# The last stage of an attention and spectral-mix kernel, issued by a written list of steps

## The chip, the cores and the metric

The kernel runs on one core of a Trainium2 chip. The metric is the device time of one execution in microseconds (us). PE is the matrix engine, PEld its loading of stationary operands, DVE the vector engine, ACT the scalar engine, POOL the GpSimd engine, and SP the engine whose queue issues transfers here. PSUM is the memory that PE writes; a bank of it holds 512 f32 numbers in each of 128 partitions, and there are eight.

## The reference, cut to what matters

Causal attention over 8 batches, 8 heads, 576 positions and 64 columns gives x of 8 x 576 x 512. Then a spectral mix and a channel mix follow:

```python
X = np.fft.rfft(x, axis=1)
Y = np.zeros_like(X)
Xr, Xi = (np.real(X[:, :n_modes]), np.imag(X[:, :n_modes]))      # n_modes = 64
Yr = np.einsum('bmd,mde->bme', Xr, w_r) - np.einsum('bmd,mde->bme', Xi, w_i)
Yi = np.einsum('bmd,mde->bme', Xr, w_i) + np.einsum('bmd,mde->bme', Xi, w_r)
Y[:, :n_modes] = Yr + 1j * Yi
y = np.fft.irfft(Y, n=S, axis=1)
u = x + y
return (u + np.maximum(u @ w_ch, 0.0)).astype(np.float32)
```

The weights w_r and w_i are 64 x 512 x 512 each, 134 MB of f32 together, and are read once.

## The kernel before, in words

The order of all instructions is written out by hand (manual_schedule, line 91): each engine runs its own in the order in which the program issues them, and semaphores hold an instruction until what it reads is written and what it overwrites has been read.

The kernel has three stages. The first, up to line 464, is the attention for 32 pairs of heads, with the Fourier transform of each finished part and the first three quarters of the mode products (`modes`) in between. The weights come in through GpSimd's DMA queue (line 204), converted to bf16.

The second stage (lines 644 to 660) works on the last quarter of the modes in eight chunks. Each chunk gives a row block of the spectrum Y, `yb`, and through `y_transposed` and `y_times_wch` its product with w_ch, `vb`; both are put into the tile `yv` by a transfer on SP's queue. Between the chunks, `work()` prepares the last stage. The output is cut into 36 tiles of 128 rows, taken two at a time: 18 pairs, numbered 0 to 17. Pairs 4 and 10 hold the last 64 rows of four batches. For each of the pairs 2 to 17 ("kept"), `x_transposed` transposes x through PSUM, `x_times_wch` multiplies it by w_ch into two PSUM banks z, and `keep` copies this product to SBUF (`z1s`). Pairs 0 and 1 (NPRE = 2) keep theirs in PSUM.

The third stage uses u @ w_ch = x @ w_ch + y @ w_ch. For each pair it needs z, the kept product plus the inverse transform of Y w_ch (`add_y` with which = 1: two matmuls of 512 columns), and u, which is x (`start_u`: an identity matmul on x_all) plus the inverse transform of Y (`add_y` with which = 0). ACT takes the relu of z into a result tile (`relu`), DVE adds u from PSUM to it, one bank at a time (`finish`, line 635), and SP issues the output transfers (line 637). How the kept product enters z is set per pair by `ways` (line 486):

```python
ways = dict(zip(kept, "esesessesesseses"))
```

"e": the product is kept as a sum of two f16 tiles (one more DVE subtraction in `keep`, line 535), and PE adds both by four identity matmuls (line 687). "s": it is kept in f32, and ACT copies it into PSUM (line 683), on which PE accumulates. There are seven "e" and nine "s". The PSUM pools of this stage are `upool` and `auxpool` with two tiles of one bank, one per half of u for even and odd pairs, and `zpool` with two tiles of two banks. `seed(i + 1)` of an "s" pair is issued ahead of `relu(i)`; otherwise the loop at line 705 goes pair by pair.

Of the kernel before, what the change touches and what calls it, by code (L numbers as in the profile page):

```python
# [18 lines left out]
def kernel(  # L19
# [85 lines left out]
    auxpool = ctx.enter_context(tc.tile_pool(name="aux_psum", bufs=2, space=PSUM))  # L105
# [332 lines left out]
    with tc.tile_pool(name="sc_psum", bufs=2, space=PSUM) as scpool, \  # L438
# [25 lines left out]
        fft(N - 1)  # L464
    load(loads_w(len(wq)))
# [12 lines left out]
    ways = dict(zip(kept, "esesessesesseses"))  # L478
# [5 lines left out]
    upool = ctx.enter_context(tc.tile_pool(name="u_psum", bufs=2, space=PSUM))  # L484
    zpool = ctx.enter_context(tc.tile_pool(name="z_psum", bufs=2, space=PSUM))

# [17 lines left out]
    def x_transposed(i):  # L504
        xts[i] = xt_sb[len(xts) % 2]
        for x, (b, T) in enumerate(pairs[i]):
            ps = upool.tile([P, DT, P], FP32, name="xt_ps", tag="u")
            for rows, bb, ident in parts(b, T):
                for dt in range(DT):
                    nc.tensor.matmul(  # L510
                        ps[:, dt, rows], x_all[: rows.stop - rows.start, dt, bb, T, :],
                        ident, start=True, stop=True, skip_group_check=True,
                    )
            nc.vector.tensor_copy(out=xts[i][:, x], in_=ps)
# [83 lines left out]
    def start_u(i):  # L598
        pool, tag = ((upool, "u"), (auxpool, "aux"))[i % 2]
        us[i] = [pool.tile([P, DM], FP32, name="u_ps", tag=tag) for x in range(2)]  # L600
        for x, (b, T) in enumerate(pairs[i]):
            for r, bb, ident in parts(b, T):
                nc.tensor.matmul(  # L603
                    us[i][x][r, :].rearrange("p (g d) -> p g d", d=P), ident,
# [11 lines left out]
    def relu(i, parts_=1):  # L616
        rs[i] = result(i)
        for x in range(parts_):
            n = 2 // parts_
            nc.scalar.activation(  # L620
                out=rs[i][:, n * x : n * x + n], in_=zs[i][:, n * x : n * x + n], func=ACTF.Relu
            )

    def finish(i):
        if ways.get(i) == "v":
            rs[i] = result(i)
        for x, (b, T) in enumerate(pairs[i]):
            o = rs[i][:, x, :]
            if ways.get(i) == "v":
                nc.vector.tensor_tensor(out=o, in0=zs[i][:, x, :], in1=z1s[i][:, x, :], op=ALU.add)  # L630
                nc.vector.scalar_tensor_tensor(
                    out=o, in0=o, scalar=0.0, in1=us[i][x], op0=ALU.max, op1=ALU.add
                )
            else:
                nc.vector.tensor_tensor(out=o, in0=us[i][x], in1=o, op=ALU.add)
# [108 lines left out]
```

The softmax here doesn't subtract the row's maximum and nothing guards it: scores larger than these inputs give would overflow.

## Time and profile before

| What | us |
|---|---|
| median of 6 runs | 461.55 (461.26 to 461.84) |
| the profiled execution, its own time | 461.7 |
| span of its profile | 459.9 |
| first matmul of the products with the last block (line 594) | 424.60 |
| last matmul of the last stage starts | 454.51 |
| last DVE add ends | 456.36 |

All places in the profile are us from the span's start. In the stretches each engine has its busy time, the number of instructions in brackets, then PE's granted clock as a share of full speed, the DMA engines' busy share and the GB/s that they moved. A group's row gives line, engine and operation, output<-inputs, shapes, the count, the busy time, the mean ns of one, and the idle time of the engine just before it with what ended it. Two instructions of one engine overlap at their ends, so that a mean duration is a little longer than the distance from one to the next.

### The profile page before, as it was taken

The page shows a single profiled execution, that of the slowest core. Times are in us where ns is not written, and L with a number is a line of the kernel's source. Part 1 is how long each engine was busy: PE and PEld are TensorE (multiplying, and loading weights), DVE is VectorE, ACT ScalarE, POOL GpSimd, SP SyncE. Part 2 cuts the span into 40 slices and gives each one's busy share as a digit, 9 for nine tenths or more (in the row PEclk, how much of TensorE's full clock was granted, in tenths as well). Part 3 has the DMA queues.
Part 4 walks back from the last instruction along what each step waited for, and adds up shares of the span by engine and source line. Part 5 has one row for each costly group of instructions (what it writes and reads, how often), then busy time and mean ns, then how long its engine had stood idle before and what let it go on. Part 6 is the DMA issues. An engine that isn't in the chain of part 4 may idle for free.

```text
span 459.9 us, 10252 instructions
## 1 busy us (share of the span) xinstructions
PE 347.5 (76%) x4177; PEld 215.5 (47%) x4177; DVE 233.0 (51%) x519; ACT 218.2 (47%) x375; POOL 183.0 (40%) x269
## 2 busy tenths in 40 slices
PE   1879988974667779857666777567869858988995
PEld 1556656653445446644444544434544424444442
DVE  7775666662434346644333433334436625562675
ACT  1585875554444437744344434444422303340895
POOL 7755555544445455344544434434432223100000
PEclk9997999998777779998777977777798979999999
DMA  9999999999999999999999999999999999994697
GB/s 177 201 203 203 201 202 203 203 204 204 204 202 203 203 201 202 204 204 203 202 202 205 205 204 204 205 204 204 204 210 210 211 215 211 213 212 94 233 311 292
DMA packets 110063, 95.16 MB, mean 207 GB/s; under 512 B 28544, under 2 KB 105216, under 8 KB 110016
## 3 DMA queue, kind: packets, MB, share of 16 engines
q0 software_dynamic: 98960, 81.81, 112.4%
q1 hardware_dynamic: 11056, 12.70, 9.1%
q8 instruction: 33, 0.54, 0.4%
q14 instruction: 14, 0.11, 0.1%
HBM read 164.66 MB, written 9.44 MB: 379 GB/s over the span
## 4 chain that ended last, share of the span: by engine, by line
DMA 62%; PE 26%; DVE 6%; issue 3%; POOL 1%; ACT 0%; SPq 0%; DVEq 0%; POOLq 0%; ACTq 0%
DMA w_sb<-in_moe_w_i_dram 43%; DMA w_sb<-in_moe_w_r_dram 13%; DMA q<-in_q_dram 5%; PE z_ps L520 4%; PE sc_ps L342 3%; PE av_ps L371 3%; PE yp L416 2%; PE sc_ps L336 2%; PE z_ps L585 2%; PE u_ps L603 2%; PE u_ps L585 2%; PE tr_ps L301 2%; PE z_ps L687 1%; PE ft_ps L395 1%; DMA qtA<-ncum_sb 1%
## 5 line engine op out<-in xcount | busy, mean ns | idle before, releaser
L350 ACT ACTIVATE p_sb<-sc_ps,cumt_sb 128x576 f16<-128x576 f32 (+1 forms) x256 | 142.2, 634 | 59.6 <-PE sc_ps L342 59.4
L204 POOL DMA_DIRECT2D w_sb<-in_moe_w_i_dram x60 | 45.2, 753 | 76.3 <-DMA w_sb<-in_moe_w_i_dram 34.5
L204 POOL DMA_DIRECT2D w_sb<-in_moe_w_r_dram x60 | 45.1, 752 | 69.6 <-DMA w_sb<-in_moe_w_r_dram 26.3
L204 POOL DMA_DIRECT2D v<-in_v_dram x72 | 50.8, 707 | 35.8 <-DMA w_sb<-in_moe_w_i_dram 10.7
L301 PE MATMUL tr_ps<-ident,q 64*64 64x64 bf16 x576 | 18.7, 219 | 58.8 <-DMA q<-in_q_dram 58.1
L336 PE MATMUL sc_ps<-negm,ident 128*128 128x256 bf16 x256 | 58.1, 315 | 0.2
L416 PE MATMUL yp<-w_sb,xs 128*32 128x512 bf16 x480 | 39.8, 417 | 16.7 <-DMA w_sb<-in_moe_w_i_dram 12.2
L304 DVE COPY qtA<-tr_ps 64x576 bf16<-64x576 bf16 x32 | 23.8, 744 | 53.8 <-PE tr_ps L301 53.8
L321 ACT ACTIVATE p<-sc_ps,cumt 128x64 f16<-128x64 f32 x32 | 10.0, 313 | 84.5 <-PE sc_ps L317 84.5
L342 PE MATMUL sc_ps<-qtB,ktB 128*128 128x512 bf16 (+2 forms) x192 | 46.3, 360 | 0.0
L371 PE MATMUL av_ps<-v,p_sb 128*128 128x65 f16 x1024 | 45.7, 200 | 0.0
L304 DVE COPY ktA<-tr_ps 64x576 bf16<-64x576 bf16 x32 | 24.0, 749 | 42.4 <-PE tr_ps L301 42.4
L301 PEld LDWEIGHTS <-q 64*64 64x64 bf16 x576 | 14.8, 130 | 61.6 <-DMA q<-in_q_dram 60.6
L371 PEld LDWEIGHTS <-p_sb 128*128 128x128 f16 x1024 | 40.6, 102 | 5.1 <-issue 1.1
L342 PE MATMUL sc_ps<-qtA,ktA 65*128 65x512 bf16 (+2 forms) x192 | 38.1, 309 | 0.3 <-DMA qtA<-ncum_sb 0.3
L520 PE MATMUL z_ps<-wch_sb,xs 128*128 128x512 f16 x144 | 36.3, 399 | 0.7 <-ACT z L540 0.7
L376 DVE TENSOR_REDUCE den<-av_ps 128x5 f32<-128x10 f32 x64 | 10.8, 169 | 47.7 <-PE av_ps L371 47.7
L416 PEld LDWEIGHTS <-xs 128*32 128x32 bf16 x512 | 21.6, 172 | 27.4 <-issue 24.1
L381 DVE TENSOR_TENSOR x_all<-av_ps,rcp 128x320 f16<-128x320 f32 x64 | 31.5, 492 | 2.2
L342 PEld LDWEIGHTS <-ktB 128*128 128x128 bf16 x192 | 23.4, 122 | 16.4 <-issue 7.7
L304 ACT COPY ktB<-tr_ps 64x576 bf16<-64x576 bf16 x32 | 20.3, 634 | 20.3 <-DVE ktA L304 19.6
L301 PE MATMUL tr_ps<-ident,k 64*64 64x64 bf16 x576 | 17.6, 211 | 15.0 <-DVE qtB L304 9.1
(90 smaller groups left out, 497.4 us busy)
## 6 DMA issues: line engine op xcount, KB each, us to landing
w_sb<-in_moe_w_r_dram POOLq DMA_DIRECT2D x60, 512.0 KB, 11.9
w_sb<-in_moe_w_i_dram POOLq DMA_DIRECT2D x60, 512.0 KB, 11.9
q<-in_q_dram POOLq DMA_DIRECT2D x32, 144.0 KB, 9.7
k<-in_k_dram POOLq DMA_DIRECT2D x32, 144.0 KB, 10.0
v<-in_v_dram POOLq DMA_DIRECT2D x72, 64.0 KB, 10.0
out_dram<-r_sb SPq DMA_DIRECT2D x16, 256.0 KB, 2.7
out_dram<-r_w SPq DMA_DIRECT2D x16, 256.0 KB, 2.5
x_all<-in_moe_w_i_dram POOLq DMA_DIRECT2D x3, 512.0 KB, 9.8
```

The costliest lines, as they stand in the source:

```text
L204: nc.gpsimd.dma_start(out=dst, in_=src)
L301: nc.tensor.transpose(ps[rows, r, :], src[rows, r, :], ident16[rows, rows])
L304: copy(out=dst[n % NQ][rows, :].rearrange("d (p r) -> d p r", r=R), in_=ps[rows].rearrange("d r p -> d p r"),)
L336: nc.tensor.matmul(ps[:, bass.ds(w * S, W)], ident16, negm[:, bass.ts(r, W)], start=True, stop=False, skip_group_check=True,)
L342: nc.tensor.matmul(ps[:, c0 : c0 + i1 - i0], keys[:, w, r, :], qt[:, i0:i1], start=False, stop=True, skip_group_check=True,)
L350: nc.scalar.activation(out=pt[:, poff[x] : poff[x] + S - w * W], in_=ps[:, w * S : (w + 1) * S - w * W], func=ACTF.Exp, bias=cumt_sb[:, x, ...
L371: nc.tensor.matmul(ps[:, I, r : r + NCH], lhsT, rhs, start=(i == 0), stop=(i == len(todo) - 1), skip_group_check=True,)
L376: nc.vector.tensor_reduce(out=den, in_=ps[:, :, 0 : VW : NCH], axis=mybir.AxisListType.X, op=ALU.add)
L381: nc.vector.tensor_tensor(out=x_all[:, g, b, :, D * h : D * h + D], in0=ps[:, :, 1 : NCH], in1=rcp.unsqueeze(2).to_broadcast([P, NT, D]), ...
L416: nc.tensor.matmul(ps[32 * cg : 32 * cg + 32, :], cols[:, c0 : c0 + 32, m], wt[(g, m // WM, ri)][:, m % WM, :], start=(x == 0), stop=(x == 3),
L520: nc.tensor.matmul(z[:, x, :], xts[i][:, x, dt, :], wch_sb[:, dt, :], start=(dt == 0), stop=(last and dt == DT - 1), skip_group_check=True,)
L585: nc.tensor.matmul(dst[x][r, :], G_sb[rows, bass.ds(T * P, r.stop - r.start)], yv[rows, bb, which, :], start=start, stop=True, skip_group_ ...
```

## The change

The third stage is issued from a list of steps, `plan`, each with a pair's number: sd (seed), z (`product`), u (`sum_u`), relu, t (`add_kept`), uc (`copy_u`) and o (`finish`, with its output transfers); a and b are halves. Within an engine the list's order is the order of its instructions. Of the 16 kept pairs one is "e", seven are "s"; four are "v" (z is made without the kept product, DVE adds the product in one pass and then does relu and the addition of u in a second, fused pass); four are "q" (DVE adds the product as for "v", ACT copies u to one of two SBUF tiles, and GpSimd takes the maximum with 0 and adds u, half by half). Each u is one tile of two banks, in a pool with one buffer for even and another for odd pairs, and DVE adds both banks in one instruction except for pairs 0 and 17. In the second stage `x_transposed` uses one two-bank tile and one copy per pair. The aux pool is closed after the attention and opened again behind the others, and closed before the second u pool is made. `keep` is unchanged, but takes its f16 branch for one pair in place of seven.

```diff
-    ways = dict(zip(kept, "esesessesesseses"))
+    ways = dict(zip(kept, "qsvsqvsqsvsqvsse"))
...
-    upool = ctx.enter_context(tc.tile_pool(name="u_psum", bufs=2, space=PSUM))
+    upool = ctx.enter_context(tc.tile_pool(name="u_psum", bufs=1, space=PSUM))
     zpool = ctx.enter_context(tc.tile_pool(name="z_psum", bufs=2, space=PSUM))
+    auxpool = ax.enter_context(tc.tile_pool(name="aux_psum", bufs=2, space=PSUM))
...
     def x_transposed(i):
         xts[i] = xt_sb[len(xts) % 2]
+        ps = upool.tile([P, 2, DT, P], FP32, name="xt_ps", tag="u")
         for x, (b, T) in enumerate(pairs[i]):
-            ps = upool.tile([P, DT, P], FP32, name="xt_ps", tag="u")
...
-            nc.vector.tensor_copy(out=xts[i][:, x], in_=ps)
+        nc.vector.tensor_copy(out=xts[i], in_=ps)
...
     def start_u(i):
-        pool, tag = ((upool, "u"), (auxpool, "aux"))[i % 2]
-        us[i] = [pool.tile([P, DM], FP32, name="u_ps", tag=tag) for x in range(2)]
+        us[i] = upools[i % 2].tile([P, 2, DM], FP32, name="u_ps", tag="u")
...
+    def relu(i, which):
+        if i not in rs:
+            rs[i] = result(i)
+        h = halves_of(i, which)
+        nc.scalar.activation(out=rs[i][:, h], in_=zs[i][:, h], func=ACTF.Relu)
+
+    def add_kept(i):
         rs[i] = result(i)
...
+        nc.vector.tensor_tensor(out=rs[i], in0=zs[i], in1=z1s[i], op=ALU.add)
+
+    def copy_u(i):
+        copied = uc[len(ucs) % 2]
+        ucs[i] = copied
+        nc.scalar.copy(out=copied, in_=us[i])
+
+    def finish(i, which):
+        h = halves_of(i, which)
+        if ways.get(i) == "q":
+            h = {"a": slice(0, 1), "b": slice(1, 2)}[which]
+        o = rs[i][:, h]
+        if ways.get(i) == "q":
+            nc.gpsimd.tensor_scalar(out=o, in0=o, scalar1=0.0, scalar2=None, op0=ALU.max)
+            nc.gpsimd.tensor_tensor(out=o, in0=o, in1=ucs[i][:, h], op=ALU.add)
+        elif ways.get(i) == "v":
+            nc.vector.scalar_tensor_tensor(
+                out=o, in0=o, scalar=0.0, in1=us[i][:, h], op0=ALU.max, op1=ALU.add
+            )
+        else:
+            nc.vector.tensor_tensor(out=o, in0=us[i][:, h], in1=o, op=ALU.add)
+        for x in range(h.start, h.stop):
+            b, T = pairs[i][x]
             for r, bb, _ in parts(b, T):
                 nc.sync.dma_start(
                     out=out[bb, bass.ds(T * P, r.stop - r.start), :], in_=rs[i][r, x, :]
...
+    ax.close()
+    upools.append(ctx.enter_context(tc.tile_pool(name="u2_psum", bufs=1, space=PSUM)))
...
+    def product(i):
+
+        if i < NPRE:
+            add_last(z_of(i), i, vb)
+            return
+        if ways[i] in "vq":
+            zs[i] = zpool.tile([P, 2, DM], FP32, name="z_ps", tag="z")
+        add_y(z_of(i), i, 1, start=ways[i] in "vq")
...
-    if ways[NPRE] == "s":
-        seed(NPRE)
-    for i in range(NPRE):
-        finish(i)
-    last = len(pairs) - 1
-    for i in range(NPRE, len(pairs)):
-        pre(i)
+    def sum_u(i):
         start_u(i)
-        add_y(us[i], i, 0)
-        if ways.get(i + 1) == "s":
-            seed(i + 1)
-        if ways[i] != "v":
-            relu(i, 2 if i == last else 1)
-        finish(i)
+        if i < NPRE:
+            add_y(u_of(i), i, 0, slice(0, GK))
+            add_last(u_of(i), i, yb)
+        else:
+            add_y(u_of(i), i, 0)
+
+
+
+    plan = """
+        z0 z1 relu0a u1 relu0b o0a relu1b o0b z2 u2 t2 sd3 uc2 o1b z3 z4 relu3b o2a u4 t4 u3 sd5
+        o4b z6 o2b z5 o3b u6 relu5b t6 u5 uc6 z7 o5b sd8 o6a u8 t7 u7 z8 o6b o7b z9 relu8b t9 u9
+        sd10 o8b z11 uc9 z10 t11 u10 relu10b o9a u11 o10b sd12 z13 o9b z12 o11b u12 relu12b t13
+        u13 z14 o12b uc13 t14 sd15 u14 o13a u15 o14b sd16 z15 o13b z16 relu15b u16 relu16b o15b
+        sd17 o16b z17 u17 relu17a relu17b o17a o17b
+    """
```

## The prediction

> **What bounds the kernel now.** I read the page first (time and chain), then the stretches of the last 35 us, the chain of work there, the groups of that stretch, and at the end single instructions. The page says that weight loading sets the length of the first nine tenths:
>
> ```profile
> span 459.9 us, 10252 instructions
> DMA 62%; PE 26%; DVE 6%; issue 3%; POOL 1%; ACT 0%; SPq 0%; DVEq 0%; POOLq 0%; ACTq 0%
> ```
>
> The change is in the rest. The stretches (busy us of each engine, granted clock, DMA share, GB/s) show PE full from 425 to 454.7, ACT close behind, DVE at 3.3 to 3.8 of 5, GpSimd empty:
>
> ```profile
> core 0: us, PE busy (x) PEld busy (x) DVE busy (x) ACT busy (x) POOL busy (x), PEclk, DMA share, GB/s
> 425.00:430.00 5.00, 5.00 (x25) 2.24 (x24) 3.27 (x6) 4.42 (x6) 0.00 (x0) 1.00 0.60 225
> 435.00:440.00 5.00, 5.00 (x24) 2.24 (x23) 3.46 (x7) 4.90 (x6) 0.00 (x0) 1.00 0.94 295
> 450.00:455.00 5.00, 4.94 (x23) 2.04 (x21) 3.70 (x6) 4.29 (x6) 0.00 (x0) 1.00 0.90 344
> ```
>
> The chain agrees: from 426.92 every piece is PE's, up to the last two adds. Two matmuls of 512 columns take 0.43, four 0.86:
>
> ```profile
> 426.92 0.86 PE z_ps L687 x4
> 427.79 0.43 PE z_ps L585 x2
> 428.22 0.43 PE u_ps L603 x2
> ...
> 454.51 0.23 PE u_ps L585
> ```
>
> The groups give the prices (count, then busy us, mean ns). The row by itself is of the stage before (340 to 425): one DVE pass over both banks of a pair.
>
> ```profile
> L635 DVE TENSOR_TENSOR r_w<-u_ps,r_w 128x512 f32<-128x512 f32 x16 | 10.3, 685 | 2.9 <-ACT r_w L620 2.7
> ...
> L620 ACT ACTIVATE r_w<-z_ps 128x1024 f32<-128x1024 f32 x8 | 8.2, 1022 | 1.7 <-PE z_ps L585 1.4 <-ACT r_sb L620 0.3
> ...
> L683 ACT COPY z_ps<-z 128x1024 f32<-128x1024 f32 x7 | 7.1, 1017 | 0.2
> L687 PE MATMUL z_ps<-z,ident16h 128*128 128x512 f16 x24 | 6.2, 379 | 0.0
> ```
>
> ```profile
> L535 DVE TENSOR_TENSOR z<-z_ps,z 128x1024 f16<-128x1024 f32 x6 | 7.3, 1224 | 12.8 <-ACT z L534 9.2 <-DMA w_sb<-in_moe_w_r_dram 3.6
> ```
>
> Two facts on the edges of the stage. The last chunk of modes starts at 419.51, while the last weights, issued at 398.50 and 21.7 us on the way, land at 420.2. And after the last add (453.88 + 2.48 = 456.36) the outputs still flow at full rate until 458.0:
>
> ```profile
> 419.51 1.36 PE L416 MATMUL yp<-w_sb,xs 128*32 128x512 bf16 x16
> ...
> 453.88 2.48 DVE L635 TENSOR_TENSOR r_sb<-u_ps,r_sb 128x512 f32<-128x512 f32 x4 [0.82 <-ACT r_sb L620]
> ```
>
> ```profile
> 456.00:457.00 1.00, 0.00 (x0) 0.00 (x0) 0.36 (x1) 0.00 (x0) 0.00 (x0) 1.00 1.06 406
> 457.00:458.00 1.00, 0.00 (x0) 0.00 (x0) 0.00 (x0) 0.00 (x0) 0.00 (x0) 1.00 1.04 404
> ```
>
> **The change, part by part.**
>
> *PE.* Seeds by matmul fall from seven pairs to one: 6 x 0.86 = 5.2 us of 27.8 go. PE would need some 22.6 us and stops being the bound.
>
> *ACT.* Before: 18 relus and 9 seeds of 1.02, 27.5 us. After: 10 relus, 7 seeds, 4 copies of u, 21.4 us. It has room.
>
> *DVE.* Before: 36 adds in 18 pairs of 1.29 (back to back), 23.2 us. After, with both banks in one pass: 8 adds (o), 8 adds of the kept product (t), 4 fused relu-and-adds, 20 passes in all, and 4 half passes for pairs 0 and 17. The trace has no f32 pass over 1024; L635's 0.645 for 512 less half its overhead gives 1.15, L535 shows 1.22; I take 1.2. Sum 20 x 1.2 + 4 x 0.65 = 26.6 us. The fused pass is a form that no row shows: bounds 1.15 and 2.4 (as two passes); I take 1.2, since nothing here prices an operation by how much arithmetic it does (relu 1.022, copy 1.017).
> So DVE becomes the bound: from 425.9, as now, without a wait it would end at 452.5.
>
> *Its waits.* I followed the list queue by queue with these rows (0.20 us from the last matmul to its reader, as for the first relu: two matmuls from 424.60 take 0.43, it starts at 425.23; 0.06 from engine to engine, as from a relu that ends at 429.27 to its add at 429.31, rounded up). The start as an example: PE goes z0, z1, u1 from 424.60 to 426.75, z2 to 427.18, u2 to 428.14 (after o0b frees u0's banks at 427.22), z3 behind seed 3 (ACT, 427.40 to 428.41) and z4, to 429.45; DVE goes o0a 425.90, o0b, t2 427.44 (0.2 late for z2), o1 428.64, t4 429.84, o4 431.09 (u4 ends at 430.58), o3 432.29, then t6, o5, t7 without a gap. Each u has one two-bank buffer per parity, so u(i) waits until u(i-2) is read: PE waits 3.8 us in all, never over 1.2. DVE waits 1.8: 0.2 for z2, 0.2 for u10, 1.1 at o15 (its relu comes late, since seed 16 stands ahead of it on ACT and waits for t14), a few hundredths behind each t. Later marks: o5 434.7, o8 439.5, o12 445.8, o15 450.5; o17b ends at 454.3. The same walk over the old order gives 456.3 (trace: 456.36). Gain 2.0 us at the last add.
>
> *GpSimd.* New: 16 passes over 128x512 in SBUF, per half of a "q" pair a max and an add. Its trace has only DMA issues (0.74) and small memsets. Lower bound of a half: two DVE passes of 0.68 = 1.36; upper: two of 1.23 = 2.46. I take 2.2, near the upper end, as no row vouches for this engine on tensors. Four pairs then occupy 429.5 to 433.9, 434.8 to 439.2, 440.6 to 445.0, 446.8 to 451.2: each done before the next is ready, all before DVE ends. Up to 2.2 a half costs 0.1 us at the end, at 2.46 0.6. The page "GPSIMD Engine Reference" of the Trainium skill (section 3.1) gives 4.5 us for an add of 2048 f32 elements, which makes an estimate of 1.1 for 512, and section 4.1 calls one-input work roughly line-rate; by that a half would be under 2.2, and the sum 0.1 lower.
> The built program also puts one instruction of another kind (ISA, line 644) ahead of the first max, behind the last weight issue (399.2). Its price is unknown: nothing if it is done by 429.5 (30 us of cover, 9 if it has to wait for the last weights), else 1 us per us, see the rivals.
>
> *SP.* Outputs leave in list order. o2a stands ahead of the four issues of o4, o2b ahead of o3, o13b ahead of o15: a late GpSimd half holds finished DVE pairs. Per issue 0.47 (0.93 for two), then 0.45 to the data.
>
> *Output transfers.* 256 KB take 0.65 us at 404 GB/s. The pairs of 64-row pieces (4 and 10) flow at some 200 GB/s (435 to 437): 2.5 us instead of 1.3. Together 16 x 1.3 + 2 x 2.5 = 25.8 us, and the outputs now come in 2 us less: the queue is nearly full. Walked in the same way the old order's flow ends at 458.5, 0.5 late, which I take off both. It then leaves 0.3 us more behind the last add than now: the flow ends at 456.2 against 458.0, -1.8.
>
> *Stage before.* Six subtractions (6 x 1.22 on DVE) go; transposes of a pair are copied by one DVE pass of 1.2 instead of two of 0.645. PE's waits for that copy (0.77 at 395.1 and at 404.9) should go; a single buffer makes x_transposed(1) wait about 0.1 more at 413. But the last chunk can't run before 420.2, and its last four matmuls ran at 420.5: gain between 0 and 0.3, I take 0.2. If the copy came late instead, PE has 0.7 us of weight wait as cover, then it costs.
>
> *Clock.* The gate halves the clock after long pauses: after idle times of 3.4 and 2.0 us (before 373.4 and 376.5) the eight matmuls of one product take 2.79 us instead of 1.89, while 1.41 us before 386.9 changed nothing. The pauses here are under 1.2 us; I count nothing. If it did fall, PE's 22.6 us would double in part; 3 us at half rate cost up to 1.5, but PE has 3.8 us of waits to lose first.
>
> **Sum.** -1.8 - 0.2 = -2.0 us. The profiled execution took 461.7 (span 459.9 and 1.8 around it), 0.15 over the median of 461.55. So 459.7 beside the profile, 459.55 beside the median; I say 459.6.
>
> **Rivals.**
> *GpSimd holds the output queue* (slower). For: SP is in order, and no row prices GpSimd on tensors. Against: 5 to 6 us between q pairs. In the walk the end moves by 0.1 at 2.2 a half, 1.3 at 2.8, 2.4 at 3.0, and from there 0.8 us per 0.1, since pair 13 then starts late and o15 to o17 (seven transfers of 0.65) queue behind it. It decides from 3.0; at 3.2, 463.4. The same comes of a late first half: each us after 430.4 is a us at the end, as the transfers have no slack; 4 us late makes 463.6. The same page (section 2.1) speaks against the change here: the first call into freshly loaded code pays about 6 us. If that fell at the first half instead of in the cover, the time would be an estimated 464.7.
>
> *Transfers take over* (no change). For: share 0.9 at 435 to 455 already, 25.8 us of transfers. If they run a few per cent below the rates above, or o2a's place leaves them idle early, of the 1.8 us one is left: 460.6.
>
> *The fused pass counts twice* (slower). Four times 1.2 more on DVE, the new bound: in the walk the span becomes 462.4, the time 463.9. It decides from 1.8 a pass (span 460.0). Against: relu costs ACT no more than copy.
>
> *More gained.* 1.15 per pass and an early o2a: 459.0. The transfers allow no more: flowing from 430.7 without a pause, they end at 455.2, a time of 458.8.
>
> **How the numbers follow.** A measurement here tells 0.2% (0.9 us) from no change: faster below 460.6, slower above 462.5. Forecast (with its better end) 0.62, range of its own 458.7 to 460.6, nearly all faster; transfers 0.16, two thirds of it within 0.2%; GpSimd 0.16, at 2.8 to 3.1 still the same or faster, else slower; fused pass 0.06, slower. Faster 0.66, same 0.17, slower 0.17. The range keeps 1 in 10 on either side: 458.7 up to the middle of the GpSimd case, 463.4.
>
> **What would show it.** Right: in the last stage PE at about 4 of 5, DVE at 4.5 to 5, and DVE in the chain; one-bank-pair passes near 1.2 (L631, L647, L651); GpSimd halves of 1.4 to 2.5, first start near 429.5; seeds by matmul only for pair 17; last add near 454.3; last chunk of modes near 419 to 420. Wrong: SP's queue waiting for GpSimd with DVE pairs finished, landing times of outputs growing above 4 us, a fused pass over 1.8, or a pause at 0.5 granted clock after 425.

## The result: slower by 0.25%, against a forecast of 0.4% faster

The changed kernel takes 463.19 us (median of 19 runs, 461.98 to 464.25), the kernel before 461.92 on the same chip (38 runs, 461.18 to 463.64). The ratio is 1.0025, with a 95% interval of 1.0018 to 1.0033: slower, by 1.2 us. I had said 459.6. The time lies in the range given, on the wrong side of no change.

The profiled execution took 463.3 us, its span is 461.5. The stretches of the changed kernel (columns as before) show that the last stage did become what the change made of it: DVE is nearly full up to 450, PE has room, GpSimd works. Then the transfers run full for 3.3 us more behind the last add (455.87 to 459.2):

```profile
430.00:435.00 5.00, 5.00 (x27) 1.66 (x26) 4.90 (x5) 3.72 (x5) 4.03 (x3) 1.00 0.50 194
435.00:440.00 5.00, 4.59 (x20) 1.84 (x19) 4.85 (x5) 3.03 (x4) 4.73 (x5) 1.00 0.89 271
...
450.00:455.00 5.00, 4.49 (x21) 1.79 (x19) 3.81 (x4) 3.85 (x5) 3.47 (x3) 1.00 1.03 395
...
456.00:457.00 1.00, 0.00 (x0) 0.00 (x0) 0.00 (x0) 0.00 (x0) 0.00 (x0) 1.00 1.07 414
457.00:458.00 1.00, 0.00 (x0) 0.00 (x0) 0.00 (x0) 0.00 (x0) 0.00 (x0) 0.65 1.04 399
458.00:459.00 1.00, 0.00 (x0) 0.00 (x0) 0.00 (x0) 0.00 (x0) 0.00 (x0) 0.50 1.07 412
```

The groups of its last stage give the new prices, first DVE's, then GpSimd's. A pass over both banks takes 1.22 whatever it computes, the fused one too; a GpSimd half takes 1.49 + 1.27, and 2.81 from one half to the next:

```profile
L651 DVE TENSOR_TENSOR r_w<-u_ps,r_w 128x1024 f32<-128x1024 f32 x4 | 4.9, 1220 | 1.1 <-ACT r_w L627 1.1
...
L647 DVE SCALAR_TENSOR_TENSOR r_sb<-r_sb,u_ps 128x1024 f32<-128x1024 f32 x2 | 2.4, 1222 | 0.2
```

```profile
L644 POOL TENSOR_SCALAR r_w<-r_w 128x512 f32<-128x512 f32 x4 | 6.0, 1491 | 0.0
...
L645 POOL TENSOR_TENSOR r_w<-r_w,xs 128x512 f32<-128x512 f32 x4 | 5.1, 1277 | 0.3
```

Two views of single instructions of the changed kernel carry the rest, PE's and SP's. At the turn from the second to the third stage, PE is through with twelve of the sixteen mode matmuls and waits 1.50 us for the last weights. After that four matmuls take 1.89 and 1.87 us (1.04 and 1.03 in the kernel before), with a granted clock of 0.5 from 423.2 to 426.6. The first relu starts at 427.22; before the change it was 425.23.

```profile
418.02 1.11 PE L417 MATMUL yp<-w_sb,xs 128*32 128x512 bf16 x12
420.63 0.66 PE L417 MATMUL yp<-w_sb,xs 128*32 128x512 bf16 x4 [1.50 <-DMA w_sb<-in_moe_w_i_dram]
...
423.20 1.89 PE L557 MATMUL v_ps<-wch_sb,yt_sb 128*128 128x512 f16 x4 [0.30 <-ACT yt_sb L551]
424.88 1.87 PE L589 MATMUL z_ps<-yv,G_sb 112*128 112x512 f16 x4
```

And on SP's queue issues stand still for GpSimd. The six of the first row end with o2b, which is ready at 436.55; the two of the second are pair 6's halves, the second ready at 442.31, while pair 7, which VectorE finished at 440.29, has its place behind it:

```profile
433.76 3.66 SPq L655 DMA_DIRECT2D out_dram<-r_sb  x6
...
439.77 2.90 SPq L655 DMA_DIRECT2D out_dram<-r_sb  x2
```

This table follows the end of the profiled executions. "Flow" is where the transfers fall below 150 GB/s for good, "last packet" the last output packet, read in slices of 0.1 us. The kernels below the first two are experiments.

| Profile of | first relu | last add ends | SP's last issue ends | flow ends | last packet | span |
|---|---|---|---|---|---|---|
| before | 425.23 | 456.36 | 456.72 | 458.0 | 458.6 | 459.9 |
| changed | 427.22 | 455.87 | 457.12 | 459.2 | 459.6 | 461.5 |
| changed, pause filled | 425.27 | 454.67 | 456.69 | 458.5 | 459.9 | 461.7 |
| GpSimd, old stage before | 425.76 | 455.39 | 456.63 | 458.4 | 459.3 | 461.2 |
| no GpSimd, old stage before | 425.41 | 455.57 | 455.92 | 457.7 | 459.0 | 460.4 |
| the same, other list | 425.08 | 454.85 | 455.36 | 457.2 | 458.1 | 459.5 |

Between "flow ends" and "last packet" 20 to 41 GB/s still move, at a DMA share around 0.06, about the share of one of the 16 engines. This tail lasts 0.1 to 0.6 us in the profiles of the old list and 0.4 to 1.4 in those of the new ones; why it is long in one profile and short in another, no run here shows. It is longest in the kernel with the pause filled:

```profile
457.00:458.00 1.00, 0.00 (x0) 0.00 (x0) 0.00 (x0) 0.00 (x0) 0.00 (x0) 0.50 1.05 404
458.00:459.00 1.00, 0.00 (x0) 0.00 (x0) 0.00 (x0) 0.00 (x0) 0.00 (x0) 0.50 0.58 221
459.00:460.00 1.00, 0.00 (x0) 0.00 (x0) 0.00 (x0) 0.00 (x0) 0.00 (x0) 0.50 0.06 23
```

From the last add to the end it is 3.1 to 3.5 us in four profiles of the old list, 4.5 to 5.3 with new lists without GpSimd work, and 5.2 to 7.0 with it.

### The profile page after: what moved, and what is told of

It reads as the page before. It is cut to its first block, busy times and chain, and to the rows that moved or that the text cites. A ratio compares the mean times of both kernels' runs of the same rounds, so it can differ in the third digit from the quotient of the medians.

```text
span 461.5 us, 10152 instructions
## 1 busy us (share of the span) xinstructions
PE 345.4 (75%) x4153; PEld 213.7 (46%) x4153; DVE 228.7 (50%) x483; ACT 212.4 (46%) x369; POOL 204.9 (44%) x285
## 5 line engine op out<-in xcount | busy, mean ns | idle before, releaser
L524 PE MATMUL z_ps<-wch_sb,xs 128*128 128x512 f16 x144 | 37.3, 407 | 0.0
L518 DVE CAST xs<-xt_ps 128x1024 f16<-128x1024 f32 x18 | 22.0, 1222 | 16.6 <-PE xt_ps L514 16.6
```

Source lines behind the costliest of these rows:

```text
L518: nc.vector.tensor_copy(out=xts[i], in_=ps)
L524: nc.tensor.matmul(z[:, x, :], xts[i][:, x, dt, :], wch_sb[:, dt, :], start=(dt == 0), stop=(last and dt == DT - 1), skip_group_check=True,)
```

## The experiments

Times are medians; the ratio is to the kernel before on the same chip, with its interval. The first four runs share one time of before (461.81), the next four another (461.68), then 461.64, 461.68 and 462.48. All edits are to the changed kernel unless it says otherwise.

My theory A was that the changed kernel loses its time in the last stage: GpSimd's halves come late, hold SP's queue, and the transfers end late. Rival B was the halved clock at the turn, with the pause ahead of it; rival D, that GpSimd slows what runs beside it. Theory E came up after the second group: the stage before has become longer or worse timed, whatever the last one does.

### Four single causes: the pause, the hold, the GpSimd half, the subtractions

```diff
+                if by_tile and cg == 2 and x == 2:   # ahead of the last four mode matmuls
+                    for k in range(6):
+                        nc.tensor.matmul(hot, ident16h, x_all[:, :, 0, 0, :], start=True, stop=True, ...)
```

> The changed kernel with six extra matmuls of 512 columns (0.215 us each at full clock, into a spare bank, read by nobody) on PE ahead of the last four mode matmuls, in the 1.5 us in which PE waits for the last weights. Theory (the pause lets the clock fall to half from 423.2 to 426.6, and the first relu is 2.0 us late, of it 1.6 by the clock): granted clock 1.00 there, first relu at 425.3 to 425.7, time 1.3 to 1.8 us under the changed kernel's 463.2, that is 461.4 to 461.9, the kernel before's. Rival (GpSimd and the output queue set the end whatever the start): first relu earlier, time within 0.4 us of 463.2.

Measured: 463.94 (462.72 to 466.68), ratio 1.0053 (1.0034 to 1.0073). In its profile the clock stays full and the first relu stands at 425.27, as before the change. The end is no earlier for that. First, the gain is met by a new wait, which the late start of the changed kernel had hidden: pair 2 has no seed any more, so its product is the first reader of v's rows in `yv`, and they are still on the way.

```profile
427.65 0.59 PE L596 MATMUL z_ps<-yv,G_sb 128*128 128x512 f16 x2 [0.69 <-DMA yv<-v_sb]
...
428.28 1.23 DVE L638 TENSOR_TENSOR r_sb<-z_ps,z 128x1024 f32<-128x1024 f32 x1 [1.09 <-PE z_ps L596]
```

So the 1.95 us by which its first relu is earlier are 1.2 at GpSimd's first half (429.68 against 430.89) and at the last add, 0.7 at the end of the flow, and nothing at the end: the tail behind the flow takes 1.4 us here and 0.4 in the changed kernel. And the six matmuls themselves take 1.47 us, which is lost wherever the weights are there in time. Filling the pause in this way is no remedy; what the halved clock costs by itself, the run does not tell.

```diff
-        for x in range(h.start, h.stop): ...        # finish: for "q" pairs no transfers any more
+    def store_q(i, which):                           # their own steps: st2b stands behind o3b,
+        store(i, {"a": slice(0, 1), "b": slice(1, 2)}[which])   # st6b behind o7b, st9b behind o11b, st13b behind o15b
```

> The changed kernel with the output transfers of the GpSimd halves issued as steps of their own, later in the list: o2b's behind o3's, o6b's behind o7's, o9b's behind o11's, o13b's behind o15's; all computation as it is. Theory (a GpSimd half of 2.8 us makes SP hold finished DVE pairs, and the transfers then queue up behind the last add, 3.3 us instead of 1.6): the pause of the transfers at 442 goes, the tail behind the last add falls by 1 us, time 0.7 to 1.2 us under 463.2. Rival (the transfers are at their rate anyway and only start late): under 0.4 us.

Measured: 463.87 (462.87 to 464.77), ratio 1.0043 (1.0030 to 1.0057). The pause of the flow at 442 is gone (406 GB/s there, 41 in the changed kernel), but the last relu now waits 1.42 us for a result buffer whose transfer is late. The hold moved, it did not go.

```diff
-            nc.gpsimd.tensor_scalar(out=o, in0=o, scalar1=0.0, scalar2=None, op0=ALU.max)
+        nc.scalar.activation(out=rs[i], in_=rs[i], func=ACTF.Relu)      # in copy_u
```

> The changed kernel with the maximum of the four GpSimd pairs taken by ACT in place, right behind the copy of u (four ACT passes of 1.0 us more), so that GpSimd only adds: 1.27 us a half instead of 2.81. Theory (the GpSimd chain of 22 us, back to back from 430.9 to 453.6, is what holds the outputs): GpSimd idles between pairs, last half done 3 to 5 us ahead of the last add, time 1.0 to 1.5 us under 463.2. Rival (ACT, with 4 us more, delays relus and u's buffers as much): within 0.4 us, and DVE waits longer for ACT than the 1.1 us at o15.

Measured: 463.0 (462.1 to 464.73), ratio 1.0023 (1.0009 to 1.0037): not told apart from the changed kernel. Its profiled execution (464.73, the longest of its twelve) has the clock at half from 415.1 to 418.5, ahead of the last chunk.

```diff
+            if i in (2, 4, 6, 9, 11, 14):       # in keep: the six subtractions, result not used
+                nc.vector.tensor_tensor(out=left, in0=zs[i], in1=z1s[i], op=ALU.subtract)
```

> The changed kernel with six subtractions put back on DVE in the stage before (z less its kept copy, into a tile that nobody reads, for pairs 2, 4, 6, 9, 11, 14), and nothing else. Theory (the stage before ran ahead because DVE had 7 us less to do, so that PE had nothing to do from 419.1 to 420.6): PE reaches the last chunk about 1 us later, the pause shrinks to under 0.8 us, the clock stays at 1.00, time 1.0 to 1.8 us under 463.2. Rival (the pause comes from the single transpose buffer or from the weights landing later, not from the subtractions): pause and clock as in the changed kernel, time within 0.4 us.

Measured: 463.89 (463.34 to 465.74), ratio 1.0043 (1.0023 to 1.0063). PE reaches the last chunk late (421.76), after waiting 1.36 us for y_sb in the chunk before. None of the four edits gave the time of before back. That does not clear the four causes, since three of the edits brought a delay of their own: the six matmuls, the wait for a buffer, the late last chunk.

### GpSimd taken out, and the stage before looked at

```diff
-    ways = dict(zip(kept, "qsvsqvsqsvsqvsse"))
+    ways = dict(zip(kept, "esvsevsesvsevsse"))      # and a list ordered for it
```

> The four pairs of GpSimd become pairs whose kept product is seeded on TensorE and whose relu is ScalarE's; everything else of the change stays, the list is ordered anew for it. TensorE gains 16 matmuls (4 x 0.86 us), VectorE keeps its 20 passes, ScalarE its count. Theory A (the changed kernel loses in the output transfers: halves that come late from GpSimd hold SyncE's queue, so the flow has gaps before 450 and then a tail behind the last addition of 3.3 us, where it was 1.64): the gaps go, the tail is 1.6 to 2.0 us again and the time is 459.3 to 460.8, below the kernel before. Rival B (the loss is the halved clock at the turn and the stage before it, both still here): 462.5 to 463.5, as the changed kernel. Rival C (VectorE's passes wait on TensorE's extra matmuls): VectorE's waits grow by 2 us or more and the time is 461.5 to 463.

Measured: 463.18 (462.22 to 464.25), ratio 1.0032 (1.0019 to 1.0045). My theory A fell as it stood: without GpSimd the kernel was as slow as with it. The time is the one that rival B expected, but the halved clock is not in this profile (463.02): the first relu stands at 425.68, and the four matmuls at the turn take 1.04 us.

The same kernel with the six matmuls ahead of the last four of the modes, as in the first run:

> As the run without GpSimd, and six matmuls of no use ahead of the last four mode matmuls, so that TensorE has no long pause there. Theory A: the clock stays full, the first relu stands at 425.2 to 425.4 and the time is 0.5 to 2 us below that of the run without GpSimd alone: 458.8 to 460. Rival B: this is the run that recovers: 459 to 460 too, but the run without the filling stays at 462.5 or above. If both runs stay at 462 or above, neither holds and the cost is at the end of the kernel.

Measured: 464.89 (463.36 to 466.15), ratio 1.0061 (1.0039 to 1.0084). In its profile the weights are in time and the six matmuls delay the last four by 1.4 us (421.87 to 423.27). The filled pause does not bring the time back here either. Whether the halved clock costs the run without GpSimd its time stays open, since this profile had no pause to fill.

```diff
-        ps = upool.tile([P, 2, DT, P], FP32, name="xt_ps", tag="u")      # in x_transposed
+    both = upool.tile([P, 2, DT, P], FP32, name="xt_ps", tag="u")        # once; each half copied alone
```

> The changed kernel, but the transposes of x are copied out one half at a time again, each half from its own bank, as before the change. If the single buffer is what leaves TensorE with pauses of 0.7 to 0.8 us at 411 to 413 and the longer one at 420, and these halve the clock: the clock stays full after 422 and the time falls by 1 to 2 us to 461.2 to 462.2. If the last weights, which land at 420 to 420.6, set the turn whatever stands ahead of them (my step for the stage before): no change, 463.0 to 463.5.

Measured: 472.04 (471.38 to 472.26), ratio 1.0218 (1.0196 to 1.0239). The edit did something else than meant: the halves are one tile, and the second half's transposes wait for the copy of the first in every pair, so that the last chunk starts at 429.26. It answers nothing about the buffer.

```profile
404.48 0.38 PE L516 MATMUL xt_ps<-ident16h,x_all 128*128 128x128 f16 x4 [1.07 <-DVE xs L520]
...
429.26 1.15 PE L417 MATMUL yp<-w_sb,xs 128*32 128x512 bf16 x16
```

The next is the kernel before with GpSimd work that nobody reads:

```diff
+        if i in (2, 5, 8, 11):
+            for x in range(2):
+                nc.gpsimd.tensor_scalar(out=idle[:, 0], in0=idle[:, 0], scalar1=0.0, scalar2=None, op0=ALU.max)
+                nc.gpsimd.tensor_tensor(out=idle[:, 0], in0=idle[:, 0], in1=idle[:, 1], op=ALU.add)
```

> The kernel before with eight halves of GpSimd work (a maximum and an addition of 128x512 each) on data that nobody reads: some 22 us of GpSimd work beside the last stage, and GpSimd's code for it. Theory A (GpSimd costs only because outputs wait for it): no change, 461.6 to 462.1, VectorE's passes stay at 0.6 us for 128x512. Rival D (GpSimd slows what runs beside it, or its code and its end lengthen the kernel's end): 462.4 to 463.5, with longer VectorE passes or with a longer stretch between the last transfer and the end than 1.9 us.

Measured: 462.56 (461.85 to 464.24), ratio 1.0019 (1.0006 to 1.0032). DVE's passes of two banks keep their 1.29, and from first relu to end its profile takes 34.5 us (425.89 to 460.4; before 34.7). So the last stage beside it is not slowed. The profile is 0.66 us late at the first relu, and 0.54 of that is there before GpSimd's added work starts: PE begins the chunk before the last at 411.45 (410.91 before the change), the first maximum runs at 421.63. Why the median is 0.9 us higher, one profile can't tell.

Now the kept products. In the changed kernel the last product kept is pair 17's, the one "e" pair, so the subtraction of `keep` stands on DVE directly ahead of the add that makes y_sb. Before the change pair 17 was "s". The edit exchanges 16 and 17, first in the changed kernel, then in the run without GpSimd, then in the kernel before:

```diff
-    order_z = list(kept)
+    order_z = list(kept[:-2]) + [kept[-1], kept[-2]]
```

> The changed kernel with the products of pairs 16 and 17 kept in the other order, so that the last one kept is pair 16, which needs one ScalarE copy and no VectorE subtraction, as the last one did before the change. In the changed kernel and its variants VectorE's subtraction (1.23 us) stands directly ahead of the addition that makes y_sb in the chunk before the last, and TensorE waits 0.54 to 1.36 us for y_sb there, where it waited 0.24 before. Theory E (this delays the last chunk in every execution in which the weights are not the last to come): the wait is 0.3 us or less, and the time falls by 0.4 to 1.1 us, to 462.1 to 462.8. Rival B (the last weights set the turn anyway, as my step said): 463.0 to 463.5, unchanged.

Measured: 463.29 (462.36 to 465.02), ratio 1.0032 (1.0019 to 1.0046). The wait for y_sb is 0.23, but nothing is gained: PE now comes to the last chunk at 417.22, waits 2.05 us for the last weights, and the clock is halved from 422.6 to 426.0.

> The kernel without GpSimd work, with the same exchange in the order of the kept products. Theory E: its wait of 1.35 us for y_sb falls to 0.3 us or less, and its time of 463.2 to 462.1 to 462.8, as in the changed kernel. If GpSimd's halves cost as well (a part of theory A), this one falls below the other by more than 0.3 us.

Measured: 463.61 (461.49 to 465.05), ratio 1.0033 (1.0018 to 1.0049). The wait for y_sb is 0.25; the spread is the widest of its group, and the profiled execution, its shortest (461.49), has a span of 459.7.

> The kernel before, with pairs 16 and 17 kept in the other order, so that pair 16, whose product is kept in two parts with a subtraction, comes last: the one piece of the change by itself. Theory E: TensorE's wait for y_sb in the chunk before the last grows from 0.24 to 0.8 to 1.4 us, and the time rises by 0.4 to 1.1 us, to 462.1 to 462.9. Rival B: no change, 461.5 to 461.9.

Measured: 462.98 (461.96 to 464.35), ratio 1.0036 (1.0023 to 1.0049). One line of the change by itself, and the wrong way round for the kernel before, costs as much as the whole change. In its profile DVE's subtraction stands ahead of y_sb:

```profile
411.69 1.22 DVE L535 TENSOR_TENSOR z<-z_ps,z 128x1024 f16<-128x1024 f32 x1 [2.08 <-ACT z L534]
412.83 0.68 DVE L429 TENSOR_TENSOR y_sb<-yp,y_acc 128x512 f16<-128x512 f32 x1
```

PE waits 1.35 us for it there:

```profile
413.56 0.40 PE L545 MATMUL yt_ps<-ident16h,y_sb 128*128 128x128 f16 x4 [1.35 <-DVE y_sb L429]
```

The same instruction in the kernel before:

```profile
412.82 0.40 PE L545 MATMUL yt_ps<-ident16h,y_sb 128*128 128x128 f16 x4 [0.24 <-DVE y_sb L429]
```

That the wait grew by 1.1 is shown. It is not the whole 1.3 of the median: the profiled execution, the shortest of the nine, is only 0.26 over the profiled one of before, and the longer ones were not profiled.

### The two halves of the change set against each other

An old stage before means here: 16 and 17 exchanged, and as many subtractions of no use put back as make seven. Without GpSimd, where four of the "q" pairs have become "e" pairs and subtract anyway:

```diff
+            if i in (4, 11):
+                nc.vector.tensor_tensor(out=left, in0=zs[i], in1=z1s[i], op=ALU.subtract)
...
+    order_z = list(kept[:-2]) + [kept[-1], kept[-2]]
```

> The last stage without GpSimd, behind a stage before like the old one: pair 16 kept last without a subtraction, and two subtractions of no use for pairs 4 and 11, so that VectorE does seven there as before the change. If the stage before is the cause (TensorE comes early to the last chunk, pauses for the last weights and finds its clock halved in a share of the executions): TensorE starts the last chunk at 419.3 or later, and the time is 461.2 to 462.0 with few executions above 463. If it is the last stage: 462.8 to 463.6 as in the runs without GpSimd so far.

Measured: 462.19 (461.38 to 463.52), ratio 1.0009 (0.9998 to 1.0019).

With GpSimd the six (2, 4, 6, 9, 11, 14) are put back:

> The changed kernel's last stage with GpSimd, behind the same old stage before (pair 16 kept last, six subtractions of no use put back). If the stage before is the whole cause: 461.2 to 462.0, as the run without GpSimd. If GpSimd's halves cost at the end too (5.2 to 7.0 us from the last addition to the end in the profiles with GpSimd, 4.5 to 5.3 without it, 3.3 to 3.5 with the list of before): 0.4 to 1.2 us above the run without GpSimd.

Measured: 463.28 (462.62 to 463.7), ratio 1.0032 (1.0021 to 1.0042). The two intervals don't overlap. With the same stage before, the kernel with GpSimd takes 1.1 us more than the one without. Not all of that is the last stage's. Every execution has its span beside its time: the medians of the spans are 461.1 and 460.4, so 0.7 us lie between the first and the last instruction. The other 0.4 lie outside: 2.10 to 2.48 us of the time in all twelve executions with GpSimd, 1.71 to 1.88 in those without, and 1.75 to 1.89 in the changed kernel, which does not pay this part. The stretches of the run with GpSimd show full transfers until 458.4:

```profile
455.00:456.00 1.00, 0.00 (x0) 0.00 (x0) 0.39 (x1) 0.00 (x0) 0.00 (x0) 1.00 1.07 412
...
457.00:458.00 1.00, 0.00 (x0) 0.00 (x0) 0.00 (x0) 0.00 (x0) 0.00 (x0) 0.87 1.05 402
458.00:459.00 1.00, 0.00 (x0) 0.00 (x0) 0.00 (x0) 0.00 (x0) 0.00 (x0) 0.50 0.45 172
```

In the one without they fall during 457, though its last add is 0.18 later:

```profile
456.00:457.00 1.00, 0.00 (x0) 0.00 (x0) 0.00 (x0) 0.00 (x0) 0.00 (x0) 1.00 1.05 406
457.00:458.00 1.00, 0.00 (x0) 0.00 (x0) 0.00 (x0) 0.00 (x0) 0.00 (x0) 1.00 0.74 283
```

The old stage before is worth 1.1 us without GpSimd (1.0033 to 1.0009, intervals that just touch) and narrows the spread from 3.6 to 2.1 us. With GpSimd it is worth nothing in the median (1.0032 both), though the spread falls from 2.7 to 1.1. So these four runs, which all keep pair 17 ahead of 16, stand at 1.0032 (GpSimd), 1.0033 (without it), 1.0032 (GpSimd, subtractions back) and 1.0009 (without it, subtractions back): the time falls only when GpSimd is out and the subtractions are back, and either alone gains nothing.

The kernel before with less work on DVE in that stage:

```diff
+            if i == 16:                              # six of seven subtractions gone
                 nc.vector.tensor_tensor(out=z1s[i][:, 1], in0=zs[i], in1=z1s[i][:, 0], op=ALU.subtract)
...
-                        zs[i][:, x, :], ident16h, z1s[i][:, y, x, :],
+                        zs[i][:, x, :], ident16h, z1s[i][:, y if i == 16 else 0, x, :],
```

> The kernel before without six of its seven subtractions; the second half of the kept product is left out, and the seed reads the first half twice, so that TensorE's work is the same. VectorE has 6 x 1.2 us less to do in the stage before. If VectorE's work there costs nothing and coming early costs nothing either (my step): 461.3 to 461.9. If TensorE comes earlier to the last chunk, pauses for the last weights and finds its clock halved: 462.2 to 463.5, slower with less work, and the profile shows a pause of 1 us or more ahead of the last four mode matmuls. If the subtractions held the stage up: 460.3 to 461.2.

Measured: 463.27 (461.7 to 464.75), ratio 1.0028 (1.0013 to 1.0043). Six passes fewer, and the kernel is slower by 1.3. The pause that was expected is there:

```profile
418.52 1.11 PE L416 MATMUL yp<-w_sb,xs 128*32 128x512 bf16 x12
420.78 0.65 PE L416 MATMUL yp<-w_sb,xs 128*32 128x512 bf16 x4 [1.15 <-DMA w_sb<-in_moe_w_i_dram]
...
423.34 1.04 PE L554 MATMUL v_ps<-wch_sb,yt_sb 128*128 128x512 f16 x4 [0.30 <-ACT yt_sb L548]
```

In this execution (461.79, its second shortest) the clock did not fall after it. So it is shown that the subtractions cost nothing and that their absence costs. That the halved clock is why, in the executions of 463 to 464.75, is argued from the profiles of the changed kernel and of the run with the kept order, and the mean granted clock of the single executions does not bear it out: the six longest (463.53 and over) have 0.866 to 0.877, the three shortest (461.88 and under) 0.869 to 0.876. One stretch of 3.4 us at half clock would lower the mean by an estimated 0.004 (1.7 of 460 us), no more than executions of one kernel differ anyway, so this speaks against the clock without ruling it out. In the kernel before with the exchanged order the longer executions do have the lower clock: 0.861 to 0.872 in the three longest, 0.875 to 0.880 in the three shortest.

The run without GpSimd and with the old stage before once more, with another list:

```diff
-        z0 z1 relu0a u1 relu0b sd2 relu1b o0a z2 sd3 o0b u2 z3 relu2b o1b u3 relu3b o2b z4 u4 ...
+        z0 z1 u1 relu0a relu0b sd2 relu1b sd3 o0a o0b z2 u2 o1b z3 u3 relu2b z4 o2b relu3b u4 ...
```

> As the run without GpSimd behind the old stage before, with another order of the list in which the outputs of pairs 2 to 5 are issued earlier and TensorE has fewer waits. Followed queue by queue with the durations of the profiles, its last addition stands 0.6 us earlier. If the end of the kernel follows the last addition: 0.4 to 0.8 us below the other run without GpSimd, 460.6 to 461.5, below the kernel before. If the transfers set the end, or the stage before does: within 0.3 us of the other run.

Measured: 461.89 (461.15 to 462.33), ratio 0.9999 (0.9989 to 1.0009): as the kernel before. It is 0.3 us below the other run without GpSimd, whose interval it overlaps, so the two lists are not told apart, and the gain of 0.4 to 0.8 us did not come. Its last add, at 454.85, is 1.5 us earlier than before the change, the end of the flow 0.8 and the end of the profile 0.4.

### The transfers

The 64-row pieces of pairs 4 and 10 went at 205 GB/s, half the full rate. The edit sends two of them as one:

```diff
+            if T == NF:
+                nc.sync.dma_start(out=out[b : b + 2, T * P : T * P + NL, :], in_=rs[i][:, x, :])
+                continue
```

> The run without GpSimd with the other list, and the 64-row pieces of pairs 4 and 10 sent two at a time (one transfer for two batches), four transfers in place of eight. If its end is set by the transfers, which run full from 452 on: the pieces go at 400 GB/s in place of 205, some 2.5 us of the flow come free, the stretch from the last addition to the end falls from 4.65 to 3.5 to 4 us, and the time is 460.6 to 461.2, below the kernel before. If the end follows the additions, or a joined transfer goes at 205 GB/s too: 461.6 to 462.1, no change.

> The changed kernel with the same joined pieces and nothing else altered. If its end is set by the transfers: the stretch from the last addition to the end falls from 5.63 to 4 to 4.6 us and the time by 1.0 to 1.6 us, to 461.6 to 462.2. If what is late are GpSimd's halves themselves, held in the order of the queue: a gain of 0.4 us at most, 462.8 to 463.2.

> The kernel before with the joined pieces. There the last stage is bound by TensorE, the flow has gaps at 451 and 454 to 455, and the queue is empty before the last pair: no change, 461.4 to 461.8, whichever theory holds of the changed kernel. A gain of over 0.5 us would say that the transfers set the end there as well.

Measured: 478.3, 481.12 and 476.34, ratios 1.0331 (1.0308 to 1.0354), 1.0400 (1.0377 to 1.0424) and 1.0291 (1.0268 to 1.0313). Every expectation was missed, by 14 us or more. In the stretches of the kernel before with joined pieces, the flow is all but dead from 435 to 440, and a transfer of the pair behind takes 12.3 us to land:

```profile
435.00:440.00 5.00, 5.00 (x24) 2.23 (x23) 3.28 (x6) 4.86 (x5) 0.00 (x0) 1.00 0.11 27
440.00:445.00 5.00, 5.00 (x29) 1.81 (x28) 3.77 (x6) 3.05 (x4) 0.00 (x0) 1.00 0.89 290
445.00:450.00 5.00, 1.80 (x9) 0.69 (x8) 0.28 (x1) 1.30 (x2) 0.00 (x0) 1.00 0.48 178
```

A joined piece has a DRAM side of 2 x 64 x 512. The Trainium skill, page "DMA: Bandwidth & Descriptors", section "Why a DMA increments its semaphore by 16 and not by 1", says that a transfer is spread over as many of the 16 engines as divide the outermost size on both sides; an outermost size of 2 leaves two. The trace agrees: in stretches of 1 us the flow is mostly 16 to 53 GB/s while the pieces go alone, and two of 16 engines that move 404 GB/s together would give an estimated 50. So the question whether the transfers set the changed kernel's end was not answered by these runs. Its own profile says this much: from 451 to 459 the flow is 395 GB/s or more in every microsecond, where the kernel before falls to 266 and 240 at 454 and 455. There the transfers have no slack left, and the last add no longer sets the end.

## Why the prediction was wrong, by its own steps

Three terms failed: the stage before, entered as a gain of 0.2; the GpSimd half, entered as 2.2 us with 0.1 at the end; and the end of the flow, entered as 1.9 us behind the last add. The step from the first relu to the last add was right.

*PE, ACT, DVE.* Right. One pass took 1.22 (I took 1.2), the fused one the same, so that rival is out; the wait at o15 is 1.05 (1.1 foreseen). From first relu to last add I had 29.1 us (425.23 to 454.3); the changed kernel took 28.65, the two runs of the table with the same last stage and a full clock at the turn 29.40 and 29.63. What these two are over is pair 2: I let z2 run at 427.18 without asking whether v's rows had landed. The old seed of four matmuls had covered that.

*GpSimd.* Right in kind, wrong in size. I took 2.2 a half between 1.36 and 2.46; it is 2.81, outside the bounds. My walk gives 1.3 us at 2.8, where I had entered 0.1; measured with a like stage before, 1.1, of which 0.7 in the span. That it comes by way of SP's queue is argued: work of GpSimd that holds no output cost the kernel before 0.9 (0.3 to 1.5). I had bounded an engine that the trace did not show by another's rows. The Trainium skill, page "GPSIMD Engine Reference", section 3.1, made an estimate of 1.1 for the add, near the measured 1.27; but the max of section 4.1, "roughly line-rate", took 1.49, longer than the two-input add. The load of its code cost nothing that shows: the first max takes 1.49 as the others, after 31.6 us of idle time, so that the 6 us of section 2.1 of that page show nowhere.

*SP and output transfers.* I had the flow end 1.9 us behind the last add; it was 3.3, and 3.8 and 3.0 in the same two runs with a full clock. SP's last issue stands 1.25 behind the last add (0.36 before the change). That the queue stood still for GpSimd is shown, but it is only a part: the new lists without GpSimd have the flow end 2.1 to 2.7 behind the last add. Of the two profiles with a like stage before, the one with GpSimd is 0.35 later at the first relu, 0.7 at the end of the flow, 0.3 at the last packet and 0.8 at the end. And with GpSimd out and the old stage before, the other list gains 1.5 at the last add and 0.4 at the end: that a gain at the last add reaches the end nearly whole (2.0 there, 1.8 in the flow) is the step that held in none of these runs.

*From the flow to the end.* I carried over 1.9 us from the profile of before. It was 2.3 here, see the last section.

*Stage before.* This is the step that failed in kind: "gain between 0 and 0.3, I take 0.2". I looked at the work that goes and at the landing of the last weights, and took any earlier arrival as a gain or as nothing. Two things were missed. The last kept product changed from "s" to "e", which put a subtraction ahead of y_sb (waits of 0.54 to 1.36 us instead of 0.24), and by itself costs the kernel before 0.36%. And an earlier arrival ends in a pause: without six subtractions the kernel before loses 0.28%. Put right one at a time in the changed kernel, neither brought the time back (1.0032 and 1.0043).

*Clock.* "I count nothing" failed. I measured pauses only inside the last stage; the one that counted stands ahead of it and was made by the step above. Nor was a limit to be read off one pair of rows: 1.41 us changed nothing in the profile of before, 1.50 was followed by half clock in the changed kernel, 1.67 was not in the run with later stores, 1.15 was not in the kernel before without subtractions, and 2.05 was in the run with the kept order. One and the same pause did both: 1.36 us of wait for y_sb was followed by half clock in the run with the relu on ACT, and not in the run with the subtractions back.

*The sum.* In the profiled execution the end is 3.6 us later than I had it (461.5 against 459.9 - 2.0): 2.2 by the start of the last stage, -0.4 up to the last add, 1.4 from there to the end of the flow, 0.4 to the end. These do not add as causes do: with GpSimd in the last stage, an early start was given back at v's rows and on SP's queue.

*Rivals.* "GpSimd holds the output queue" (0.16) is a part of what the last stage did. At 2.8 a half I had counted it as "still the same or faster", since my other gains were to pay for it; but those gains did not reach the end, and the stage before, priced as a gain, was a cost. "Transfers take over" can't be told from it by these runs; the full flow from 451 to 459 fits both.

What is left open: why the executions of one kernel spread over 1.9 to 4.0 us when the stage before is short and over 1.1 to 2.1 in the three runs with the old one (the kernel before itself, in more executions, over 2.3 to 2.8). The halved clock fits some of it, but no execution from the upper end of the range was profiled in the two runs that would tell most, the one without GpSimd in the other kept order and the kernel before without subtractions. Also open: why GpSimd work that nobody reads costs 0.9 us, and so how much of GpSimd's cost in the changed kernel is the queue's.

## What to carry to other kernels

Work that ends before a fixed arrival may cost time when it is removed: if the engine ahead of it then waits, look at the length of its pause and at the clock behind it, and look at which small instruction now stands directly ahead of the one that everybody waits for. An engine with no row of its own is bounded from above only by running it; until then, price its lateness together with every transfer that stands behind it in the queue. And when the last engine gets faster than the output queue, the gain is to be read at the last packet, not at the last add.

## What was not expected of the hardware

- GpSimd takes 1.49 us for a maximum with a constant over 128x512 f32 and 1.27 for an addition of two such tiles: the operation with fewer inputs is the slower one, in all eight halves.
- Pauses of PE of 1.50 and 2.05 us were followed by 3.4 us of halved clock in two kernels, a pause of 1.67 was not in a third. The Trainium skill, page "TensorE: Matmul & The Clock Gate", Part 1, speaks of an idle window of about 3.4 us that runs freely, so that the point of transition varies from run to run; the varying agrees with these rows, the length of idle time that it takes does not, if one counts single pauses.
- From the last output packet to the end of the profile it is 1.8 to 1.9 us in seven profiles and 1.3 to 1.4 in the other ten with separate pieces. All seven have GpSimd's maximum and addition as the way of four pairs; with the addition alone it was 1.4, with both on data that nobody reads 1.4. The half microsecond is shown, its cause isn't.
- A transfer of 256 KB with an outermost size of 2 on its DRAM side went at mostly 16 to 53 GB/s and held up the transfers behind it, 14 to 18 us for four of them, where one with 128 rows outermost goes at 404.
